# Two wq matrices loaded by one DMA of 96 rows each, in a two-problem decode attention kernel

## The chip, the cores and the metric

One core of one Trainium2 chip runs the whole kernel. The metric is device microseconds of one execution, as the median of several. A profiled execution gives a page and a trace; its span begins and ends a little inside the time of that execution.

## The reference, cut to what matters

Two independent problems, A and B, have the same shapes; their outputs are laid side by side. Everything is bf16.

```python
B, Sq, D = 2, 1, 576
Hq, Hkv, Sk, Dh = 32, 16, 16384, 128
W = min(4096, max(256, Sk // 4))             # 4096
q = (x @ wq)                                 # wq is 576 x 4096; 2 batches, 32 heads of 128
k = k_cache[:, :, Sk - W:, :]                # the last 4096 rows, each kv head shared by 2 q heads
v = v_cache[:, :, Sk - W:, :]
p = softmax(q k^T * Dh ** -0.5)
return (p v) @ wo                            # wo is 4096 x 576
```

For each problem that is 2 x 16 caches of 4096 x 128 for K and as many for V, wq of 4.7 MB and wo of 4.7 MB: 153 MB to read in all, with two rows of x per problem against them.

## The kernel before, in words

The kernel is a list of operations written in Python and emitted in order, engine by engine; each operation names those it depends on, and a small planner turns that into semaphore waits. The engines are PE (matmuls), DVE, ACT, POOL and SP; SP issues nearly all DMAs, in order, and waits in that order too.

**Slabs.** Four kv heads' worth of K (or V) make a slab: 128 partitions of 32768 bytes, 4 MB. There are 16 slabs of K and 16 of V. They go through a ring of four slots in SBUF (`ring`, `NR = 4`), one DMA each. The order is the list `stream`: wq of A, wq of B, K0, K1, V0, K2, V1 and so on (V13 is the one slab moved, and the last V slab comes in two pieces). Stream element n takes slot n mod 4, and its DMA (L256) waits for the last reader of element n - 4. So V0 waits for the last matmul of q that reads wq of A, K2 for the last that reads wq of B, V1 for the last transpose of K0. The weights wo come in parts between slabs (L291), the last ones (L277) at the very end of the queue.

**wq and x.** 576 rows of wq are cut into 512 and 64. The 512 go into a ring slot as 128 partitions of 4 rows (L265). The 64 go into `wqr` (L263), each row cut into two halves so that 128 partitions of 4096 bytes are filled. x of A is loaded from ACT's queue, x of B from SP's, behind wq of A. L380 doubles the 64 rest columns of x, five matmuls at L375 transpose x (4 rows) into a PSUM bank, L389 (ACT) and L397 (DVE, with the mask maskP of L382) write it, spread into a zeroed tile, to `xT`, which holds the stationary operands of q.

**q.** `do_qpair` (L425 to L456) makes q for two groups at a time into four PSUM banks: per pair 16 matmuls of 128x512 on the ring slot and four on `wqr` (a matmul's line is L450, or the helper's L188 where the stationary operand is kept). There are four pairs, 80 matmuls. Per group, ACT copies the row out (L465 or L470), DVE transposes it (L475), ACT keeps it (L483).

**Per slab pair.** DVE transposes each K slab in four parts into one of three buffers `xt` (L515), PE makes scores from it (L540), then come maximum, exponential (ACT, L585), and a transpose of the weights (L593). PE multiplies them with the V slab (L631) into the bank `ACC`; ACT evicts that to `acc_sb` (L643). For all groups but the last, POOL folds the evicted slab in three steps (mask L650, add L653, add L658) and a matmul per slab (L671) sums over partitions. In the last group (slabs 14 and 15) there is no fold: four matmuls per slab sum it (L678). DVE scales the result, redistribution and projection matmuls (L786, L790) finish it. Softmax sums go through `rsel` (POOL, L600).

**The end.** After slab 13, the list has: sum of slab 13, projection of a group (L786, eight pairs), redistribution, sum of slab 14, another projection of eight pairs, then the two pieces of the last V slab (L631), its sum, its projection with the last weights (L790), and output.

**Small parts.** Masks are reduced from a 128x128 identity, which POOL makes (L207, L208); L213 makes it in fp32. The tiles that only the q phase needs (`early`) share SBUF with the second half of `wob`, the place of wo.

Of the kernel before, what the change touches and what calls it, by code (L numbers as in the profile page):

```python
# [59 lines left out]
def build_kernel(nc, probs, out, cfg=None):  # L60
# [25 lines left out]
    NFC = D // 128  # L86
    DREM = D - 128 * NFC
    assert DREM * 2 == 128 and NFC * HD == SLABW
    HH = HD // 2
    NXC = NFC + 2  # L90
# [23 lines left out]
    with es:  # L114
        sb = lambda name, shape, dt: es.enter_context(nc.sbuf_tensor(name, shape, dt))
        ring = sb("ring", [128, NR, SLABW], BF16)
        xt = sb("xt", [128, NKT, 2048], FP32)
        wob = sb("wob", [128, NSW, NOUT], BF16)
        used = [0]

        def early(shape):
            n = 1
            for d_ in shape:
                n *= d_
            a = wob[:, NSW // 2:NSW, :].rearrange("p s n -> p (s n)")[:, used[0]:used[0] + n]
            used[0] += n
            assert used[0] <= NSW // 2 * NOUT
            names = "abc"[:len(shape)]
            return a if len(shape) == 1 else a.rearrange("p (%s) -> p %s" % (" ".join(names), " ".join(names)), **dict(zip(names, shape)))
        wqr = early([NPROB, HH])  # L130
        qrow = early([1024])
        qtr = early([1024])
        xT = early([NXC, NPROB, 128])
        x_sb = early([D])[0:NPROB * Bb]
        x_dup = early([DREM, 2])[0:NPROB * Bb]
# [20 lines left out]
        masks = sb("masks", [128, 30], BF16)  # L156
        maskS, mask16D, maskA, mask4S, maskJ, maskP = (masks[:, a_:b_] for a_, b_ in ((0, 8), (8, 16), (16, 20), (20, 24), (24, 28), (28, 30)))
# [21 lines left out]
        wq_sem = sem("wq")  # L179
# [22 lines left out]
        def load_x(P, eng):  # L202
# [4 lines left out]
        p_ones_b = S.add("pool", lambda e: e.memset(ones_b[:], 1.0), [], "ones_b")  # L207
        p_ident_b = S.add("pool", lambda e: e.affine_select(ident_b[:], ones_b[:], [[-1, 128]], ALU.is_equal, 0.0,  # L208
                                                           base=0, channel_multiplier=1), [p_ones_b], "ident_b")
        p_zxT = S.add("dve", lambda e: e.memset(xT[:].rearrange("c h p w -> c (h p w)").bitcast(FP32), 0.0), [], "zero_xT")  # L210
        p_zq = S.add("dve", lambda e: e.memset(zq[:].rearrange("d p z w -> d (p z w)").bitcast(FP32), 0.0), [], "zero_zq")
        p_ones_f = S.add("dve", lambda e: e.memset(ones_f[:], 1.0), [], "ones_f")
        p_ident_f = S.add("pool", lambda e: e.affine_select(ident_f[:], ones_f[:], [[-1, 128]], ALU.is_equal, 0.0,  # L213
                                                           base=0, channel_multiplier=1), [p_ones_f], "ident_f")
# [13 lines left out]

        slab_dma = {}
        pieces = []  # L230
        reader = {}
        wq_dma = {}
# [6 lines left out]
        def issue_slab(n):  # L239
# [7 lines left out]
            r = n % NR  # L247
# [11 lines left out]
        def issue_wq(n, P):  # L259
            wqP = probs[P][3]  # L260
            r = n % NR
            deps = [reader[n - NR]] if n >= NR else []
            wq_dma[P] = dma_op("sp", wq_sem, 1, lambda e: e.dma_start(  # L263
                wqr[:, P, :], wqP[NFC * 128:D, :].rearrange("r (h n) -> r h n", h=2)).then_inc(wq_sem, 16), [], "wqr%d" % P)
            slab_dma[n] = dma_op("sp", ring_sem[r], 1, lambda e: e.dma_start(  # L265
                ring[:, r, :], wqP[0:NFC * 128, :].rearrange("(p s) n -> p (s n)", s=NFC)).then_inc(ring_sem[r], 16), deps, "wq%d" % P)

            if P == 0:
                for P_ in range(1, NPROB):
                    x_dma[P_] = load_x(P_, "sp")  # L270
# [96 lines left out]
        def f_xT(e, bank):  # L367
            last = None
            NB = NPROB * Bb
            for ch in range(NFC + 1):  # L370
                if ch < NFC:
                    src = x_sb[0:NB, 0:NFC * 128].rearrange("b (p s) -> b s p", s=NFC)[:, ch, :]
                else:
                    src = x_dup[0:NB, :, :].rearrange("b r t -> b (r t)")
                last = e.matmul(bank[:, ch * 4 * NB:(ch + 1) * 4 * NB], src, ident_b[0:NB, 0:NB].rearrange(  # L375
                    "k (p b) -> k p b", b=Bb).unsqueeze(2).broadcast_to([NB, NPROB, 4, Bb]), start=True, stop=True)
            return last
        issue_until(0)
        init_small()
        x_cd = S.add("dve", lambda e: e.tensor_copy(  # L380
            x_dup[:], x_sb[:, NFC * 128:D].unsqueeze(2).broadcast_to([NPROB * Bb, DREM, 2])), list(x_dma.values()), "xdup")
        init["maskP"] = S.add("dve", lambda e: e.tensor_reduce(  # L382
            maskP[:], ident_b[:].rearrange("d (r t) -> d t r", t=2), AX.X, ALU.max), [p_ident_b], "maskP")

        n_x, bank_x, op_xT = tb_job(f_xT, "xT", list(x_dma.values()) + [x_cd, p_ident_b])

        def f_xev(e):
            NB = NPROB * NFC * 4
            return e.activation(  # L389
                xT[:, 0:NFC].rearrange("c h p (a w) -> c (h p a) w", a=4)[:, :, 0:Bb],  # L390
                bank_x[:, 0:NB * Bb].rearrange("c (q b) -> c q b", b=Bb),
                ACTF.Copy)
        op_xev = S.add("act", f_xev, [op_xT, p_zxT], "xev")
        NB_ = NPROB * 4 * Bb

        def f_xev2(e):
            return e.tensor_tensor(  # L397
                xT[:, NFC:NXC].rearrange("c h p (a w) -> c h (p a) w", a=4)[:, :, :, 0:Bb],
                bank_x[:, NFC * NB_:(NFC + 1) * NB_].rearrange("c (q b) -> c q b", b=Bb).unsqueeze(1).broadcast_to([128, 2, NPROB * 4, Bb]),
                maskP[:].unsqueeze(2).unsqueeze(3).broadcast_to([128, 2, NPROB * 4, Bb]), ALU.mult)  # L400
        op_xev = S.add("dve", f_xev2, [op_xev, op_xT, init["maskP"]], "xev2")
        tb_consumer[n_x] = op_xev

# [20 lines left out]
        def do_qpair(i):  # L424
# [5 lines left out]
            mine = lambda ch: [b for b in range(4) if ch < NFC or b % 2 == ch - NFC]  # L430
            order = [NFC, NFC + 1] + list(range(NFC))
            if Gs[0] % GPP:
                order = order[::-1]
            todo_ = [(ch, b) for ch in order for b in mine(ch)]
# [4 lines left out]
            for g in range(2):  # L439
                def fn(e, part=todo_[(0, ends[0])[g]:ends[g]]):  # L440
                    last = None
                    for ch, b in part:
                        c0 = (b % 2) * HH + 512 * (Gs[b // 2] % GPP)
                        w_ = ring[:, nq % NR, ch * HD + c0:ch * HD + c0 + 512] if ch < NFC else wqr[:, P, c0 - (b % 2) * HH:c0 - (b % 2) * HH + 512]
                        start, stop = seen[b] == 0, seen[b] == NFC
                        seen[b] += 1
                        if q_first[0] == (P, ch):
                            last = matmul_again(e, q_first[1], banks[b], w_, start, stop, False)
                        else:
                            last = q_first[1] = e.matmul(banks[b], xT[:, ch, P, :], w_, start=start, stop=stop)  # L450
                            q_first[0] = (P, ch)
                    return last
                before = [q_free.get((i - 1, b)) for b in range(4)] if g else []
                op = S.add("pe", fn, [slab_dma[nq], op_xev] + list(wq_dma.values()) + prev + before, "q%d" % Gs[g])
# [53 lines left out]
        def do_X(s, u):  # L508
# [4 lines left out]
            if i >= NKT:  # L513
                deps.append(Sop[divmod(i - NKT, NU)])
            Xop[(s, u)] = S.add("dve", lambda e: e.transpose(  # L515
                xt[:, i % NKT, :].rearrange("k (j w) -> k j w", w=64),
                ring[:, n % NR, :].bitcast(FP32).rearrange("k (j q w) -> k q j w", q=4, w=64)[:, u]),
# [78 lines left out]
        def do_rsel(G):  # L596
            d = [chain[(2 * G, "exp")], chain[(2 * G + 1, "exp")], init["maskS"]]
            if G >= 1:
                d.append(chain[(G - 1, "tot")])
            chain[(G, "rsel")] = S.add("pool", lambda e: e.tensor_tensor(  # L600
# [17 lines left out]
        def do_PV(D_, rounds, wait):  # L618
# [7 lines left out]
            def f(e):  # L626
                last = None
                for jr in rounds:
                    for cb in range(4):
# [3 lines left out]
                                        ring[:, n % NR, j0_ * 128:(j0_ + 4) * 128],  # L633
# [5 lines left out]
            if rounds[-1] == last_r:  # L639
# [5 lines left out]
                if not by_group(G) or (D_ % 2 == 0 and G < NG - 2):  # L645
                    return
                l0, l1 = (0, 2) if G < NG - 2 else (D_ % 2, D_ % 2 + 1)
                a_ = acc_sb[:, l0:l1, :]
                v = a_.rearrange("k l (j d) -> k l j d", j=4)
                t = S.add("pool", lambda e: e.tensor_tensor(  # L650
                    v, v, maskJ[:].unsqueeze(1).unsqueeze(3).broadcast_to([128, l1 - l0, 4, 128]), ALU.mult),
                    [acc_ev[2 * G + l] for l in range(l0, l1)] + [init["maskJ"]], "accm%d" % D_)
                t = S.add("pool", lambda e: e.tensor_tensor(a_[:, :, 0:256], a_[:, :, 0:256], a_[:, :, 256:512], ALU.add),  # L653
                          [t], "acca%d" % D_)
                d = [t]
                if G >= 1:
                    d.append(comb[2 * G - 1])
                t = S.add("pool", lambda e: e.tensor_tensor(  # L658
                    acc_r[:, l0:l1, :], a_[:, :, 0:128], a_[:, :, 128:256], ALU.add), d, "accr%d" % D_)
                for l in range(l0, l1):  # L660
                    acc_r_ev[2 * G + l] = t

        def do_comb(D_):
            if by_group(D_ // 2):
# [8 lines left out]
                n, bank, comb[D_] = tb_job(fg, "comb%d" % D_, [acc_r_ev[D_ - 1], acc_r_ev[D_], init["maskS"]])  # L673
            else:
# [230 lines left out]
        do_comb(D_)  # L905
        do_norm(D_)
# [117 lines left out]
```

## Time and profile before

| what | value |
|---|---|
| median of 3 runs | 362.77 us (362.70 to 362.87) |
| the profiled execution | 363.02 us |
| its span | 361.8 us |
| busy: PE, DVE, ACT, POOL | 218.6, 200.9, 68.2, 35.3 us |
| DMA read | 153.10 MB, 423 GB/s over the span |
| queue q1 | 6476 packets, 98.8% of 16 engines' span |
| first wq issue, first V issue | 0.79 us, 26.99 us |
| last weights landed | 359.71 us |

Busy time is per engine; engines overlap. A DMA is cut into packets, here one per row of a partition, and these are shared over sixteen DMA engines, each with its own line of packets to work off. The DMA row of the page gives, for 40 equal slices of the span, how full these engines are, in tenths. The chain of waits is followed back from the last instruction: at each step to what released it. A landing mark in the trace is the moment at which one DMA engine reports its share of a transfer done.

### The profile page before, as it was taken

To read this page: it belongs to the slowest core of one execution; us is meant where nothing else is said; L and a number is where in the kernel's file an instruction comes from. 1 tells how busy PE (TensorE), PEld (TensorE's weight loads), DVE (VectorE), ACT (ScalarE), POOL (GpSimd) and SP (SyncE) were. 2 spreads that over 40 slices of the span, in tenths; PEclk is the share of its full clock that TensorE was granted. 3 is DMA by queue.
4 is the path that set the end of the run, shared out by engine and by line. 5 is a ranking of instruction groups with operands and counts; after the bars stand their busy time and mean duration, and the time that the engine had idled before them with its cause. 6 is when DMAs were issued, how large, how long until landed. Compare 5 with 4: busy or idle time off the path is not lost.

```text
span 361.8 us, 2730 instructions
## 1 busy us (share of the span) xinstructions
PE 218.6 (60%) x1318; PEld 55.8 (15%) x945; DVE 200.9 (56%) x175; ACT 68.2 (19%) x149; POOL 35.3 (10%) x55
## 2 busy tenths in 40 slices
PE   0399195763747207466574737766867707657786
PEld 0010021120111101112120201212121201211132
DVE  4112599846647019283756658392919239079931
ACT  1036502130203002103020203020201203002131
POOL 1000000004000400001300040002100040200020
PEclk9999689997889857969698978899898978969999
DMA  8999999999999999999999999999999999999996
GB/s 348 421 449 406 464 406 437 431 408 453 415 442 438 428 424 438 429 428 438 417 446 422 435 428 442 426 435 428 424 424 440 431 424 433 431 438 428 438 409 248
DMA packets 6491, 153.27 MB, mean 424 GB/s; under 512 B 712, under 2 KB 1232, under 8 KB 1616
## 3 DMA queue, kind: packets, MB, share of 16 engines
q1 hardware_dynamic: 6476, 153.10, 98.8%
q8 instruction: 9, 0.15, 0.2%
q14 instruction: 2, 0.02, 0.0%
q10 hardware_dynamic: 4, 0.00, 0.0%
HBM read 153.10 MB, written 0.00 MB: 423 GB/s over the span
## 4 chain that ended last, share of the span: by engine, by line
DMA 72%; DVE 17%; PE 7%; ACT 3%; SPq 1%; issue 0%
DMA ring<-in_B_k_cache_dram 34%; DMA ring<-in_A_k_cache_dram 27%; DVE xt L515 14%; DMA wob<-in_B_wo_dram 8%; DMA wob<-in_B_x_dram 3%; PE st L188 3%; PE st L540 3%; ACT wob L465 1%; DVE wob L475 1%; ACT qk L483 1%; PE st L450 1%; DVE m L550 1%; ACT wob L470 1%; DVE nM L563 0%; SPq L252 0%
## 5 line engine op out<-in xcount | busy, mean ns | idle before, releaser
L515 DVE STREAM_TRANSPOSE xt<-ring 128x2048 f32<-128x2048 f32 x64 | 145.3, 2284 | 86.6 <-DMA ring<-in_A_k_cache_dram 49.8
L540 PE MATMUL st<-xt,zq 128*128 128x512 bf16 x256 | 111.6, 436 | 122.6 <-DVE xt L515 98.1
L188 PE MATMUL st<-xt,zq 128*128 128x512 bf16 x256 | 110.1, 430 | 0.0
L540 PEld LDWEIGHTS st<-xt,zq 128*128 128x128 bf16 x256 | 27.1, 106 | 216.3 <-DVE xt L515 113.5
L631 PE MATMUL acc<-ring,pC 128*32 128x512 bf16 x512 | 32.5, 381 | 1.2 <-DMA ring<-in_B_v_cache_dram 1.2
L568 ACT ACTIVATE nMrep<-nM 1x128 f32<-1x128 f32 x16 | 4.9, 308 | 146.9 <-DVE nM L563 146.9
L643 ACT ACTIVATE acc_sb<-acc 128x512 bf16<-128x512 f32 x16 | 9.5, 596 | 79.9 <-PE acc L631 79.9
L593 DVE STREAM_TRANSPOSE pC<-pR 128x1024 bf16<-128x1024 bf16 x16 | 19.6, 1223 | 3.7 <-ACT pR L585 2.1
L650 POOL TENSOR_TENSOR acc_sb<-acc_sb,masks 128x1024 bf16<-128x1024 bf16 (+1 forms) x8 | 13.4, 1679 | 66.6 <-ACT acc_sb L643 66.6
L550 DVE TENSOR_REDUCE m<-st 128x1 f32<-128x1024 f32 x16 | 19.0, 1190 | 1.4 <-PE st L188 1.4
L502 POOL TENSOR_TENSOR zq<-qk,masks 128x128 bf16<-128x128 bf16 x16 | 6.3, 398 | 136.2 <-PE st L188 114.4
L585 ACT ACTIVATE pR<-st,bias_sb 128x1024 bf16<-128x1024 f32 x16 | 17.8, 1114 | 0.5
L475 DVE STREAM_TRANSPOSE wob<-wob 128x512 f32<-128x512 f32 x8 | 5.7, 711 | 20.3 <-ACT wob L465 12.9
L415 ACT ACTIVATE st<-maskB 128x1024 f32<-128x1024 bf16 x16 | 16.5, 1032 | 1.6 <-POOL rsel L600 0.4
L786 PE MATMUL ot<-wob,Rsb 128*2 128x512 bf16 x56 | 15.2, 390 | 0.0
L631 PEld LDWEIGHTS acc<-ring,pC 128*32 128x32 bf16 x512 | 12.4, 96 | 15.9 <-issue 3.2
L600 POOL TENSOR_TENSOR rsel<-masks,rsum 128x16 f32<-128x16 bf16 x8 | 1.7, 216 | 108.0 <-ACT pR L585 108.0
L188 PE MATMUL tb<-wob,Rsb 128*2 128x64 bf16 x56 | 10.9, 195 | 0.0
L375 PE MATMUL tb<-wob 4*128 4x16 bf16 x5 | 0.3, 179 | 14.5 <-DVE wob L380 14.5
L653 POOL TENSOR_TENSOR acc_sb<-acc_sb 128x512 bf16<-128x512 bf16 (+1 forms) x8 | 8.2, 1029 | 0.6
L188 PE MATMUL st<-ring,wob 128*128 128x512 bf16 x24 | 7.9, 445 | 0.0
L579 ACT ACTIVATE bias_sb<-tb 128x1 f32<-128x1 f32 x16 | 2.7, 171 | 24.8 <-PE tb L573 24.8
(89 smaller groups left out, 99.5 us busy)
## 6 DMA issues: line engine op xcount, KB each, us to landing
ring<-in_A_k_cache_dram SPq DMA_DIRECT2D x8, 4096.0 KB, 30.4
ring<-in_A_v_cache_dram SPq DMA_DIRECT2D x8, 4096.0 KB, 32.5
ring<-in_B_k_cache_dram SPq DMA_DIRECT2D x8, 4096.0 KB, 28.4
ring<-in_B_v_cache_dram SPq DMA_DIRECT2D x7, 4096.0 KB, 32.8
wob<-in_A_wo_dram SPq DMA_DIRECT2D x1, 4608.0 KB, 43.3
ring<-in_A_wq_dram SPq DMA_DIRECT2D x1, 4096.0 KB, 12.7
ring<-in_B_wq_dram SPq DMA_DIRECT2D x1, 4096.0 KB, 22.6
ring<-in_B_v_cache_dram SPq DMA_DIRECT2D x1, 3072.0 KB, 25.5
```

The costliest lines, as they stand in the source:

```text
L188: return e.add_instruction(mybir.InstMatmult(name=nc.get_next_instruction_name(), engine=i.engine, ins=[e.lower_ap(rhs), i.ins[1]], outs=[ ...
L415: chain[(s, "fill")] = S.add("act", lambda e: e.activation(ST[s % 2][:, :].rearrange("k (h j) -> k h j", h=2), maskB[:].unsqueeze(1).broad ...
L475: chain[(G, "qtr")] = S.add("dve", lambda e: e.transpose(qtr[:].bitcast(FP32), qrow[:].bitcast(FP32)), evs, "qtr%d" % G)
L515: Xop[(s, u)] = S.add("dve", lambda e: e.transpose(xt[:, i % NKT, :].rearrange("k (j w) -> k j w", w=64), ring[:, n % NR, :].bitcast(FP32) ...
L540: first = last = e.matmul(bank, zq[:, p4, s % NZQ, w0:w0 + 128], mv, start=False, stop=stop, skip_group_check=True)
L550: chain[(s, "max")] = S.add("dve", lambda e: e.tensor_reduce(m1[:, 0:1], ST[s % 2][:, :], AX.X, ALU.max), d, "max%d" % s)
L585: chain[(s, "exp")] = S.add("act", lambda e: e.activation(pR[:, :], ST[s % 2][:, :], ACTF.Exp, bias=bias_sb[:, 0:1], scale=SCALE, accum_ou ...
L593: chain[(s, "pC")] = S.add("dve", lambda e: e.transpose(pC[:, s % NPT, :, :].rearrange("k j c -> k (j c)"), pR[:, :]), d, "pC%d" % s)
L631: last = e.matmul(ACC[32 * cb:32 * cb + 32, 0:512], pC[:, D_ % NPT, j0_:j0_ + 4, :].rearrange("k j c -> k (j c)"), ring[:, n % NR, j0_ * 1 ...
L643: acc_ev[D_] = S.add("act", lambda e: e.activation(acc_sb[:, D_ % 2, :], ACC[:, :], ACTF.Copy), d, "accev%d" % D_)
L650: t = S.add("pool", lambda e: e.tensor_tensor(v, v, maskJ[:].unsqueeze(1).unsqueeze(3).broadcast_to([128, l1 - l0, 4, 128]), ALU.mult), [a ...
L786: first = e.matmul(OT[0:Bb, 0:NB0], l_, wob[:, w0 + s_, 0:NB0], start=start and begin, stop=end, skip_group_check=True)
```

## The change

wq of a problem comes by a single DMA: 576 = 96 x 6, so 96 partitions of 6 rows, 49152 bytes each, in place of 128 partitions of 32768 and 128 of 4096. As a row is now wider than a ring slot, `xt`, `ring` and `wob` become one tile `big`: wq of A lies over slot 0 and the end of `xt` ahead of it, wq of B over slot 3 and the start of `wob` behind it; the slots are taken in the order 0, 3, 1, 2. The first three transposes of K0 into `xt` also wait for the last reader of wq of A.

q sums six products of 96 rows: 24 matmuls per pair, 96 in all, with contraction over 96 partitions.

x is turned without PE: ACT copies its rows apart (`x_s`), DVE transposes 32 x 192 three times (`x_t`), ACT spreads it into `xT`, once per problem. `x_dup`, maskP and the five matmuls go.

Slab 14's accumulator is folded by POOL, in place, with the same three steps as the others; one matmul in place of four sums it.

Three small operations leave POOL: ones_b goes to DVE, the fp32 identity is copied by ACT, and the first group's `rsel` is made by two ACT operations.

```diff
-    NFC = D // 128
+    NFC = 6
+    DP = D // NFC
+    EXT = NFC * HD - SLABW
+        RING0 = NKT * 4096
+        WOB0 = RING0 + NR * SLABW
+        big = sb("big", [128, WOB0 + NSW * NOUT], BF16)
...
+        wqv = [big[0:DP, RING0 - EXT:RING0 + SLABW], big[0:DP, WOB0 - SLABW:WOB0 + EXT]]
...
-        p_ones_b = S.add("pool", lambda e: e.memset(ones_b[:], 1.0), [], "ones_b")
+        p_ones_b = S.add("dve", lambda e: e.memset(ones_b[:], 1.0), [], "ones_b")
+        p_zxs = S.add("dve", lambda e: e.memset(x_s[:].rearrange("b s p -> b (s p)").bitcast(FP32), 0.0), [], "zero_xs")
-        p_ident_f = S.add("pool", lambda e: e.affine_select(ident_f[:], ones_f[:], [[-1, 128]], ALU.is_equal, 0.0,
-                                                           base=0, channel_multiplier=1), [p_ones_f], "ident_f")
+        p_ident_f = S.add("act", lambda e: e.activation(ident_f[:], ident_b[:], ACTF.Copy), [p_ident_b], "ident_f")
...
+        slot = [(0, 3, 1, 2)[n % NR] for n in range(len(stream))]
...
-            wq_dma[P] = dma_op("sp", wq_sem, 1, lambda e: e.dma_start(
-                wqr[:, P, :], wqP[NFC * 128:D, :].rearrange("r (h n) -> r h n", h=2)).then_inc(wq_sem, 16), [], "wqr%d" % P)
             slab_dma[n] = dma_op("sp", ring_sem[r], 1, lambda e: e.dma_start(
-                ring[:, r, :], wqP[0:NFC * 128, :].rearrange("(p s) n -> p (s n)", s=NFC)).then_inc(ring_sem[r], 16), deps, "wq%d" % P)
+                wqv[P], wqP.rearrange("(p s) n -> p (s n)", s=NFC)).then_inc(ring_sem[r], 16), [], "wq%d" % P)
...
+        x_cp = S.add("act", lambda e: e.activation(
+            x_s[0:NB], x_sb[:, :].rearrange("b (p s) -> b s p", s=NFC), ACTF.Copy), list(x_dma.values()) + [p_zxs], "xcp")
+        for i_ in range(DP // 32):
+            op_xt = S.add("dve", lambda e, i_=i_: e.transpose(
+                x_t[32 * i_:32 * i_ + 32], x_s[:, :, 32 * i_:32 * i_ + 32]), [x_cp], "xtr%d" % i_)
+        for P_ in range(NPROB):
+            op_xev = S.add("act", lambda e, P_=P_: e.activation(
+                xT[0:DP, :, P_].rearrange("c h (a w) -> c h a w", a=4)[:, :, :, 0:Bb],
+                x_t[:, :, Bb * P_:Bb * P_ + Bb].unsqueeze(2).broadcast_to([DP, NFC, 4, Bb]), ACTF.Copy), [op_xt, p_zxT], "xev%d" % P_)
...
-            order = [NFC, NFC + 1] + list(range(NFC))
+            order = list(range(NFC))
...
-            todo_ = [(ch, b) for ch in order for b in mine(ch)]
+            todo_ = [(ch, b) for ch in order for b in range(4)]
...
-                            last = q_first[1] = e.matmul(banks[b], xT[:, ch, P, :], w_, start=start, stop=stop)
+                            last = q_first[1] = e.matmul(banks[b], xT[0:DP, ch, P, :], w_, start=start, stop=stop)
...
-            if i >= NKT:
-                deps.append(Sop[divmod(i - NKT, NU)])
+            deps.append(Sop[divmod(i - NKT, NU)] if i >= NKT else reader[pos[("Q", 0)]])
...
+            if G == 0:
+                for l in range(2):
+                    chain[(G, "rsel")] = S.add("act", lambda e, l=l: e.activation(
+                        rsel[:, l, :], maskS[:], ACTF.Copy, scale=rsum[:, l:l + 1]), d, "rsel%d_%d" % (G, l))
+                return
...
+            elif D_ < ND - 1:
+                n, bank, comb[D_] = tb_job(lambda e, bank: e.matmul(
+                    bank[:, 0:8], acc_sb[:, 0, 0:128], maskS[:, :], start=True, stop=True), "comb%d" % D_, [acc_r_ev[D_], init["maskS"]])
...
         do_comb(D_)
+        do_fold(ND - 2, 0, 1)
         do_norm(D_)
```

`do_fold` holds the three POOL steps that stood in `do_PV`.

More of the change, by code (lines that the diff above doesn't have):

```diff
@@ L85, in build_kernel @@
     GPP = SPP // 2
-    NFC = D // 128
-    DREM = D - 128 * NFC
-    assert DREM * 2 == 128 and NFC * HD == SLABW
+    NFC = 6
+    DP = D // NFC
     HH = HD // 2
-    NXC = NFC + 2
+    EXT = NFC * HD - SLABW
+    assert D == DP * NFC and DP % 16 == 0 and 0 < EXT <= 2 * 4096
     NOUT = wo0.shape[1]
@@ L115, in build_kernel @@
         sb = lambda name, shape, dt: es.enter_context(nc.sbuf_tensor(name, shape, dt))
[L116 to L119, printed above, removed]
+        RING0 = NKT * 4096
+        WOB0 = RING0 + NR * SLABW
+        big = sb("big", [128, WOB0 + NSW * NOUT], BF16)
+        xt = big[:, 0:RING0].bitcast(FP32).rearrange("k (n w) -> k n w", n=NKT)
+        ring = big[:, RING0:WOB0].rearrange("k (n w) -> k n w", n=NR)
+        wob = big[:, WOB0:WOB0 + NSW * NOUT].rearrange("k (s n) -> k s n", n=NOUT)
+        wqv = [big[0:DP, RING0 - EXT:RING0 + SLABW], big[0:DP, WOB0 - SLABW:WOB0 + EXT]]
+        used = [EXT]
         def early(shape):
@@ L124, in early @@
                 n *= d_
-            a = wob[:, NSW // 2:NSW, :].rearrange("p s n -> p (s n)")[:, used[0]:used[0] + n]
+            a = big[:, WOB0 + used[0]:WOB0 + used[0] + n]
             used[0] += n
-            assert used[0] <= NSW // 2 * NOUT
+            assert used[0] <= NSW * NOUT
             names = "abc"[:len(shape)]
             return a if len(shape) == 1 else a.rearrange("p (%s) -> p %s" % (" ".join(names), " ".join(names)), **dict(zip(names, shape)))
-        wqr = early([NPROB, HH])
         qrow = early([1024])
         qtr = early([1024])
-        xT = early([NXC, NPROB, 128])
+        xT = early([NFC, NPROB, 128])
         x_sb = early([D])[0:NPROB * Bb]
-        x_dup = early([DREM, 2])[0:NPROB * Bb]
+        x_s = early([NFC, DP])[0:32]
+        x_t = early([NFC, 32])[0:DP]
         ident_b = early([128])
@@ L155, in build_kernel @@
         Rsb = [sb("Rsb%d" % n_, [128, Bb, n], BF16) for n_, n in enumerate((32, 16))]
-        masks = sb("masks", [128, 30], BF16)
-        maskS, mask16D, maskA, mask4S, maskJ, maskP = (masks[:, a_:b_] for a_, b_ in ((0, 8), (8, 16), (16, 20), (20, 24), (24, 28), (28, 30)))
+        masks = sb("masks", [128, 28], BF16)
+        maskS, mask16D, maskA, mask4S, maskJ = (masks[:, a_:b_] for a_, b_ in ((0, 8), (8, 16), (16, 20), (20, 24), (24, 28)))
         mask16S = sb("mask16S", [128, 16], BF16)
@@ L178, in build_kernel @@
         ring_sem = [sem("ring%d" % r) for r in range(NR)]
-        wq_sem = sem("wq")
         wo_sem = [sem("wo%d" % r) for r in range(2)]
@@ L231, in build_kernel @@
         reader = {}
-        wq_dma = {}
         wo_dma = {}
@@ L246, in issue_slab @@
             src = src_t.rearrange("b h s d -> (b h) s d")[g::SPP, Sk - W:Sk, :].rearrange("c (r j) d -> r c (j d)", r=32)
-            r = n % NR
+            r = slot[n]
             deps = [reader[n - NR]] if n >= NR else []
@@ L260, in issue_wq @@
             wqP = probs[P][3]
-            r = n % NR
-            deps = [reader[n - NR]] if n >= NR else []
-            wq_dma[P] = dma_op("sp", wq_sem, 1, lambda e: e.dma_start(
-                wqr[:, P, :], wqP[NFC * 128:D, :].rearrange("r (h n) -> r h n", h=2)).then_inc(wq_sem, 16), [], "wqr%d" % P)
+            r = slot[n]
             slab_dma[n] = dma_op("sp", ring_sem[r], 1, lambda e: e.dma_start(
-                ring[:, r, :], wqP[0:NFC * 128, :].rearrange("(p s) n -> p (s n)", s=NFC)).then_inc(ring_sem[r], 16), deps, "wq%d" % P)
+                wqv[P], wqP.rearrange("(p s) n -> p (s n)", s=NFC)).then_inc(ring_sem[r], 16), [], "wq%d" % P)
             if P == 0:
@@ L365, in init_small @@
                 ident_r[:], ident_b[:].rearrange("d (a r) -> d r a", a=4), AX.X, ALU.max), [p_ident_b], "ident_r")
[L367 to L377, printed above, removed]
@@ L378, in build_kernel @@
         issue_until(0)
         init_small()
[L380 to L401, printed above, removed]
@@ L402, in build_kernel @@
-        tb_consumer[n_x] = op_xev
+        NB = NPROB * Bb
+        x_cp = S.add("act", lambda e: e.activation(
[7 more added lines that the diff above has]
+                x_t[:, :, Bb * P_:Bb * P_ + Bb].unsqueeze(2).broadcast_to([DP, NFC, 4, Bb]), ACTF.Copy), [op_xt, p_zxT], "xev%d" % P_)
@@ L429, in do_qpair @@
             banks = q_banks(i)
-            mine = lambda ch: [b for b in range(4) if ch < NFC or b % 2 == ch - NFC]
-            order = [NFC, NFC + 1] + list(range(NFC))
+            order = list(range(NFC))
             if Gs[0] % GPP:
                 order = order[::-1]
-            todo_ = [(ch, b) for ch in order for b in mine(ch)]
+            todo_ = [(ch, b) for ch in order for b in range(4)]
             seen = {b: 0 for b in range(4)}
@@ L442, in fn @@
                     for ch, b in part:
-                        c0 = (b % 2) * HH + 512 * (Gs[b // 2] % GPP)
-                        w_ = ring[:, nq % NR, ch * HD + c0:ch * HD + c0 + 512] if ch < NFC else wqr[:, P, c0 - (b % 2) * HH:c0 - (b % 2) * HH + 512]
-                        start, stop = seen[b] == 0, seen[b] == NFC
+                        c0 = ch * HD + (b % 2) * HH + 512 * (Gs[b // 2] % GPP)
+                        w_ = wqv[P][:, c0:c0 + 512]
+                        start, stop = seen[b] == 0, seen[b] == NFC - 1
                         seen[b] += 1
@@ L453, in do_qpair @@
                 before = [q_free.get((i - 1, b)) for b in range(4)] if g else []
-                op = S.add("pe", fn, [slab_dma[nq], op_xev] + list(wq_dma.values()) + prev + before, "q%d" % Gs[g])
+                op = S.add("pe", fn, [slab_dma[nq], op_xev] + prev + before, "q%d" % Gs[g])
                 reader[nq] = op
@@ L512, in do_X @@
             deps = [slab_dma[n]]
-            if i >= NKT:
-                deps.append(Sop[divmod(i - NKT, NU)])
+            deps.append(Sop[divmod(i - NKT, NU)] if i >= NKT else reader[pos[("Q", 0)]])
             Xop[(s, u)] = S.add("dve", lambda e: e.transpose(
                 xt[:, i % NKT, :].rearrange("k (j w) -> k j w", w=64),
-                ring[:, n % NR, :].bitcast(FP32).rearrange("k (j q w) -> k q j w", q=4, w=64)[:, u]),
+                ring[:, slot[n], :].bitcast(FP32).rearrange("k (j q w) -> k q j w", q=4, w=64)[:, u]),
                 deps, "X%d_%d" % (s, u))
@@ L632, in f @@
                                         pC[:, D_ % NPT, j0_:j0_ + 4, :].rearrange("k j c -> k (j c)"),
-                                        ring[:, n % NR, j0_ * 128:(j0_ + 4) * 128],
+                                        ring[:, slot[n], j0_ * 128:(j0_ + 4) * 128],
                                         start=(jr == 0), stop=(jr == last_r))
@@ L644, in do_PV, with do_fold @@
                 G = D_ // 2
[L645 to L661, printed above, removed]
+                if G < NG - 2 and D_ % 2:
+                    do_fold(D_, 0, 2)
+                elif G == NG - 2:
+                    do_fold(D_, D_ % 2, D_ % 2 + 1)
+        def do_fold(D_, l0, l1):
+            G = D_ // 2
+            a_ = acc_sb[:, l0:l1, :]
+            v = a_.rearrange("k l (j d) -> k l j d", j=4)
+            t = S.add("pool", lambda e: e.tensor_tensor(
+                v, v, maskJ[:].unsqueeze(1).unsqueeze(3).broadcast_to([128, l1 - l0, 4, 128]), ALU.mult),
+                [acc_ev[2 * G + l] for l in range(l0, l1)] + [init["maskJ"]], "accm%d" % D_)
+            t = S.add("pool", lambda e: e.tensor_tensor(a_[:, :, 0:256], a_[:, :, 0:256], a_[:, :, 256:512], ALU.add),
+                      [t], "acca%d" % D_)
+            d = [t]
+            if 1 <= G < NG - 1:
+                d.append(comb[2 * G - 1])
+            o_ = acc_r[:, l0:l1, :] if by_group(G) else a_[:, :, 0:128]
+            t = S.add("pool", lambda e: e.tensor_tensor(
+                o_, a_[:, :, 0:128], a_[:, :, 128:256], ALU.add), d, "accr%d" % D_)
+            for l in range(l0, l1):
+                acc_r_ev[2 * G + l] = t
         def do_comb(D_):
```

## The prediction

> **What bounds the kernel now.** I read the page first, its second and third parts.
>
> ```profile
> span 361.8 us, 2730 instructions
> ...
> DMA  8999999999999999999999999999999999999996
> GB/s 348 421 449 406 464 406 437 431 408 453 415 442 438 428 424 438 429 428 438 417 446 422 435 428 442 426 435 428 424 424 440 431 424 433 431 438 428 438 409 248
> ...
> q1 hardware_dynamic: 6476, 153.10, 98.8%
> ```
>
> The DMA row is at nine tenths or more in all slices but the first and the last, and the packets of queue q1 fill 98.8% of sixteen engines' span, 0.988 x 361.8 = 357.5 us. Nothing else is near: PE 60%, DVE 56%. So a compute edit is worth nothing while the queue stays filled, and whatever lengthens the busiest engine's packets is paid in full. The end confirms it, in the chain of waits:
>
> ```profile
> 331.87 27.84 DMA wob<-in_B_wo_dram
> 359.71 0.04 issue
> 359.75 0.31 PE st L790 x2
> 360.06 0.02 issue
> 360.08 0.45 DVE pR L823
> ```
>
> The last weights, issued 27.84 us earlier, land at 359.71; 0.04 + 0.31 + 0.02 + 0.45 us of work and the output DMA follow. Time is (first packet) + (packets of the slowest engine) + (this tail).
>
> Third, SP's timeline shows how long the queue runs on if a slab is issued late:
>
> ```profile
> 0.79 0.40 SPq L263 DMA_DIRECT2D wob<-in_A_wq_dram  x1
> ...
> 1.72 0.31 SPq L203 DMA_DIRECT2D wob<-in_B_x_dram  x1
> ...
> 3.00 1.26 SPq L256 DMA_DIRECT2D ring<-in_A_k_cache_dram  x2
> 26.99 0.54 SPq L256 DMA_DIRECT2D ring<-in_A_v_cache_dram  x1
> 36.04 0.54 SPq L256 DMA_DIRECT2D ring<-in_A_k_cache_dram  x1
> 50.67 0.54 SPq L256 DMA_DIRECT2D ring<-in_A_v_cache_dram  x1
> ```
>
> By the trace's landing marks the second K slab is in at 44.43, V0 at 54.14 and K2 at 63.93. So V0, issued at 26.99, had 17.4 us to spare; K2 (36.04) 18.1 us; V1 (50.67) 13.3 us.
>
> **The wq load.** The trace's packet records give the price by size: 4096 B take 159 ns, 32768 B 1215 ns (medians), 36864 B 1364 ns, a semaphore packet 9 ns. From the smallest to the largest that is (1364 - 159) / 32768 = 0.0368 ns per byte, so 49152 B take 1364 + 12288 x 0.0368 = 1816 ns (an estimate). A problem's wq is now 128 packets of 32768 B and 128 of 4096 B, on each engine 8 x (1215 + 159) + 2 x 9 = 11010 ns. Afterwards it is 96 packets; six on each engine, if evenly shared, are 6 x 1816 + 9 = 10905 ns. Two problems: -0.21 us. The bytes are the same.
>
> Nothing in the trace shows a big load on fewer than 128 partitions, so this share is bounded from both sides. Below: -0.21 us and up to 0.1 us of the slow first packets (the 256 of 4096 B average 176 ns against 159, most of that the first arrival, which stays), so -0.3. Above: every packet at half pace, 6 x 1816 more per problem, +21.8 us. [...] The nearest row is the second x load, two rows in neighbouring partitions: its landing marks are two, at 13.69 and 14.18 us, so neighbours went to two engines, by count and not by place. I take the even split.
>
> [...]
>
> **The head.** Two small issues leave SP's queue (0.40 and 0.34 us of issuing), but the first big one takes the place of the first small one at 0.79, so the first packet (1.71 us) does not move: 0. The x of B stays behind the first wq and lands at about 14.1. What follows it now costs, in the chain,
>
> ```profile
> 14.20 0.23 DVE wob L380
> ...
> 14.47 0.34 PE tb L375 x5
> ...
> 14.83 0.23 ACT wob L389
> ...
> 15.09 0.20 DVE wob L397
> ...
> 15.42 0.59 PE st L450
> ```
>
> 1.24 us from landing to q's first matmul. Afterwards: a copy on ACT of 4 x 576, about 0.64 us (the 128x512 ones take 0.59, the 128x1024 ones 1.01); three DVE transposes of 32 x 192 bf16, at most 3 x 0.36 (the 128x1024 bf16 one takes 1.22); two ACT copies of 48 elements at 0.22 (the 64-element one). That is 2.2 us with gaps, +0.9. Then q has 24 matmuls per pair of groups in place of 20. The first 14 matmuls run at 0.43 us, the rest at 0.216, with the granted clock 1.00 throughout; 16 more cost 16 x 0.216 = 3.5 us in all, 8 x 0.216 = 1.7 of it ahead of V0's issue and at most 3.5 ahead of K2's. So V0 goes out some 2.6 us later and K2 up to 4.4: hidden by the 17.4 and 18.1 us above. V1 waits for DVE's transposes of K0, which begin after the q chain; 4.4 of its 13.3 us go. The new wait of the first transposes on q's second pair is nothing: q ends near 30, the transposes of K0 begin near 42. If that cover were gone, the price would be the delay, up to 4.4 us.
>
> POOL, DVE and ACT trades (ones_b, a memset of 128x288 f32, ident_f, the first rsel as two ACT rows of about 0.2 us instead of one POOL row of 0.22): before 14 us all three wait for x, and rsel falls at 74.35 us with two whole slabs still queued (issued at 61.36 and 66.57). 0.
>
> **The tail.** Slab 14's fold puts three POOL rows between its eviction and its sum. The row pattern is slab 13's:
>
> ```profile
> 346.92 1.04 POOL L650 TENSOR_TENSOR acc_sb<-acc_sb,masks 128x512 bf16<-128x512 bf16 x1 [0.27 <-ACT acc_sb L643]
> ...
> 348.04 0.67 POOL L653 TENSOR_TENSOR acc_sb<-acc_sb 128x256 bf16<-128x256 bf16 x1
> ...
> 348.79 0.42 POOL L658 TENSOR_TENSOR acc_r<-acc_sb 128x128 bf16<-128x128 bf16 x1
> ```
>
> From 346.92 to the matmul that uses it (349.27) 2.35 us pass. Slab 14's eviction ends at 349.04 + 0.60 = 349.64, so its matmul can start at 349.71 + 2.35 = 352.06; it stood at 351.92. Queued behind it on PE are eight pairs of projection matmuls, to 354.2, then the last slab's PV, which waits for its first piece until 354.34 and idles 1.01 us before the second piece at 356.87. So +0.14 us, up to 0.6 if DVE's 0.43 us mask product blocks POOL, go into that idle time: 0. Three matmuls fewer save 0.2 us of the same idle time: 0.
>
> **Sum.** -0.21 - 0.05 (middle of 0 to 0.1). The profiled execution took 363.02 us, its span 361.8 and 1.2 around it; 363.02 - 0.26 = 362.76. The median shown is 362.77, 0.25 below that execution: 362.5.
>
> **Rivals.**
>
> [...] 362.77 + 7.05 = 369.8. [...] Chance 27%.
>
> *The paths also collide.* If engines that meet on one path stay in step, packets run at half pace for longer; between 7 and the 21.8 us above, 372 to 384. Against it: the longest 32768 B packet of the trace takes 1.75 us, and the marks of whole slabs stay 0.5 us apart early on. 12%.
>
> *A late q phase or fold reaches the end.* The price is 4.4 us at the most, 0.5 likelier. Against it: covers of 9 us and more in the head, 1 us in the tail. 6%.
>
> *The load is not one packet per row.* The largest seen is 36864 B. Halved rows would add 12 x 9 ns: within my forecast.
>
> *More is gained.* The sixteen last marks lie between 357.81 and 359.71; if the late engines are relieved by chance, 0.8 to 1.5 us, 361.3 to 362.0. 7%.
>
> **How the numbers follow.** Forecast 48%, 362.5, its own range 362.0 to 363.3. What this kernel's measurement can tell from no change is about 0.2%, 0.73 us, so the forecast counts as the same. Slower 27 + 12 + 6 = 45%, faster 7%. The range runs from 362.0 to 371.5: it takes in the first rival and leaves out the collisions (12%) and the chance gain (7%).
>
> **What would show it.** Right: 6124 packets on q1 (6476 less 256 of 4096 B, 64 big ones and 2 x 16 semaphore packets), its share at 98.8% still, wq of A landed by 14.1 and of B by 25, V0 issued near 29.6, the second slice at 420 GB/s. [...] Wrong by the tail: a POOL row ending later than the PV's first piece. A matmul of V's last piece released by something other than its DMA would overturn the reasoning on covers.

## The result and the profile after

The changed kernel takes 385.15 us (384.81 to 385.69, 6 runs) against 362.76 us (362.63 to 362.87) for the kernel before: a ratio of 1.062, 95% interval 1.0606 to 1.0634. That is 22.4 us more, outside the range of the forecast. The profiled execution took 385.23 us with a span of 384.0.

The page of the changed kernel, the parts that were read first in the forecast:

```profile
span 384.0 us, 2734 instructions
...
DMA  9897999999999999999999999999999999999996
GB/s 236 174 246 164 263 420 420 427 435 434 434 437 432 439 437 422 427 423 428 437 430 437 435 430 430 427 435 427 427 432 430 434 416 445 434 437 427 430 418 251
...
q1 hardware_dynamic: 6124, 153.10, 98.8%
```

Three things are to be seen. The packets are 6124, as counted, and the bytes the same. The DMA row is as full as before. But for the first five slices (48 us) the GB/s row stands at 164 to 263 where it stood at 348 to 464: the engines are busy, and move about half as much. After that the two kernels are alike.

By stretches: from and to, length, the busy us and the count of PE, of its weight loads, of DVE, ACT and POOL, then PE's granted clock, the DMA share and GB/s (1.00 is a full share; a packet counts where it starts):

```profile
2.00:25.00 23.00, 0.00 (x0) 0.00 (x0) 3.09 (x13) 0.96 (x2) 0.00 (x0) 1.00 1.02 216
25.00:47.00 22.00, 13.78 (x48) 1.29 (x11) 4.66 (x9) 7.56 (x25) 0.76 (x2) 0.96 0.92 203
47.00:60.00 13.00, 12.40 (x48) 1.19 (x11) 1.42 (x2) 3.70 (x10) 0.00 (x0) 0.81 0.98 421
```

The issue lists say the same of each load; the last column is the time from issue to landing. First the larger part of each wq in the kernel before, then each wq after:

```profile
ring<-in_A_wq_dram SPq DMA_DIRECT2D x1, 4096.0 KB, 12.7
ring<-in_B_wq_dram SPq DMA_DIRECT2D x1, 4096.0 KB, 22.6
...
big<-in_A_wq_dram SPq DMA_DIRECT2D x1, 4608.0 KB, 24.5
big<-in_B_wq_dram SPq DMA_DIRECT2D x1, 4608.0 KB, 46.0
```

By the packet records, the 192 packets of 49152 bytes took 3.70 us on average (3.08 to 4.02), where the forecast had 1.816. The sum closes: 12 packets per engine x (3.696 - 1.816) - 0.21 = +22.35 us, and the measured ratio's interval is 22.0 to 23.0 us. The 192 packets start in twelve groups of sixteen, 3.1 to 3.8 us apart, which fits one packet on each engine per group. All sixteen engines were equally late: the landing marks of wq of A lie within 0.8 us (24.57 to 25.34).

The rest of the program shifted behind it. SP's timeline:

```profile
0.79 0.38 SPq L265 DMA_DIRECT2D big<-in_A_wq_dram  x1
...
1.59 0.32 SPq L265 DMA_DIRECT2D big<-in_B_wq_dram  x1
1.95 1.25 SPq L259 DMA_DIRECT2D big<-in_A_k_cache_dram  x2
42.18 0.54 SPq L259 DMA_DIRECT2D big<-in_A_v_cache_dram  x1
60.35 0.53 SPq L259 DMA_DIRECT2D big<-in_A_k_cache_dram  x1
74.08 0.54 SPq L259 DMA_DIRECT2D big<-in_A_v_cache_dram  x1
```

V0 is issued at 42.18, but K1 lands at 66.8 by its last landing mark, so the queue never ran dry. The end of the chain of waits:

```profile
380.82 1.11 PE st L777 x14
381.94 0.03 issue
381.97 0.31 PE st L777 x2
382.30 0.45 DVE pR L810
```

The chain now ends through PE, without the wait for the last weights. Their last landing mark is at 381.92, where that PE work ends: the two are level. In the timeline PE's last two groups of weight loads, at 381.65 and 381.96, still waited 0.24 and 0.23 us for those weights. From the last mark to the end of the span are 2.05 us, as before.

### The profile page after: what moved, and what is told of

It reads as the page before. It is cut to its first block, busy times and chain, and to the rows that moved or that the text cites. A ratio compares the mean times of both kernels' runs of the same rounds, so it can differ in the third digit from the quotient of the medians.

```text
span 384.0 us, 2734 instructions
## 1 busy us (share of the span) xinstructions
PE 227.5 (59%) x1325; PEld 56.5 (15%) x937; DVE 201.9 (53%) x177; ACT 70.3 (18%) x154; POOL 36.8 (10%) x55
## 3 DMA queue, kind: packets, MB, share of 16 engines
q1 hardware_dynamic: 6124, 153.10, 98.8%
## 4 chain that ended last, share of the span: by engine, by line
DMA 66%; DVE 15%; PE 14%; ACT 2%; POOL 1%; issue 0%; SPq 0%
DMA big<-in_B_k_cache_dram 23%; DMA big<-in_A_k_cache_dram 23%; DVE big L489 13%; DMA big<-in_B_wq_dram 12%; DMA big<-in_B_v_cache_dram 8%; PE st L191 5%; PE st L514 4%; PE acc L610 2%; PE ot L773 1%; DVE big L450 1%; DVE m L524 1%; PE st L425 1%; ACT big L440 1%; ACT big L445 1%; ACT st L391 0%; ACT qk L458 0%
## 5 line engine op out<-in xcount | busy, mean ns | idle before, releaser
L489 DVE STREAM_TRANSPOSE big<-big 128x2048 f32<-128x2048 f32 x64 | 145.3, 2284 | 83.4 <-DMA big<-in_A_k_cache_dram 48.2
L514 PE MATMUL st<-big,zq 128*128 128x512 bf16 x256 | 112.8, 441 | 117.9 <-DVE big L489 93.1
L191 PE MATMUL st<-big,zq 128*128 128x512 bf16 x256 | 110.9, 433 | 0.0
L514 PEld LDWEIGHTS st<-big,zq 128*128 128x128 bf16 x256 | 27.3, 107 | 212.8 <-DVE big L489 107.8
L610 PE MATMUL acc<-big,pC 128*32 128x512 bf16 x512 | 34.3, 395 | 0.5 <-DMA big<-in_B_v_cache_dram 0.5
L425 PE MATMUL st<-big 96*128 96x512 bf16 x12 | 6.3, 522 | 33.8 <-ACT big L376 28.4
L450 DVE STREAM_TRANSPOSE big<-big 128x512 f32<-128x512 f32 x8 | 5.7, 712 | 31.0 <-ACT big L440 23.0
L633 POOL TENSOR_TENSOR acc_sb<-acc_sb,masks 128x1024 bf16<-128x1024 bf16 (+1 forms) x9 | 14.5, 1612 | 77.8 <-ACT acc_sb L622 77.8
L773 PE MATMUL ot<-big,Rsb 128*2 128x512 bf16 x56 | 15.9, 402 | 0.0
L610 PEld LDWEIGHTS acc<-big,pC 128*32 128x32 bf16 x512 | 13.0, 98 | 15.6 <-issue 4.5
L191 PE MATMUL st<-big 96*128 96x512 bf16 x36 | 14.0, 514 | 0.0
L373 DVE STREAM_TRANSPOSE big<-big 32x192 bf16<-32x192 bf16 x3 | 1.1, 368 | 21.6 <-ACT big L370 21.5
L191 PE MATMUL tb<-big,Rsb 128*2 128x64 bf16 x56 | 11.1, 199 | 0.0
```

Of the source, the lines that this page charges most:

```text
L191: return e.add_instruction(mybir.InstMatmult(name=nc.get_next_instruction_name(), engine=i.engine, ins=[e.lower_ap(rhs), i.ins[1]], outs=[ ...
L425: last = q_first[1] = e.matmul(banks[b], xT[0:DP, ch, P, :], w_, start=start, stop=stop)
L450: chain[(G, "qtr")] = S.add("dve", lambda e: e.transpose(qtr[:].bitcast(FP32), qrow[:].bitcast(FP32)), evs, "qtr%d" % G)
L489: Xop[(s, u)] = S.add("dve", lambda e: e.transpose(xt[:, i % NKT, :].rearrange("k (j w) -> k j w", w=64), ring[:, slot[n], :].bitcast(FP32 ...
L514: first = last = e.matmul(bank, zq[:, p4, s % NZQ, w0:w0 + 128], mv, start=False, stop=stop, skip_group_check=True)
L610: last = e.matmul(ACC[32 * cb:32 * cb + 32, 0:512], pC[:, D_ % NPT, j0_:j0_ + 4, :].rearrange("k j c -> k (j c)"), ring[:, slot[n], j0_ * ...
```

## The experiments

Two microkernels load and compute nothing else; five kernels are variants of the two that are compared. Each microkernel ran once. Times of loads are from the packet records, from the first packet's start to the last one's end. A load alone has its first arrival in it: 128 rows took 1.1 to 1.3 us more than eight packets' median price, so the GB/s below are lower than in a full queue.

**Which property of the load is it?** The microkernel `loads` issues one load at a time, each waited for, from a list of (source, first partition, rows, elements per row):

```python
nc.sync.dma_start(slots[i % n_slot][p0:p0 + n, 0:w], src).then_inc(sems[i], 16)
nc.sync.wait_ge(sems[i], 16)
```

The theories are COUNT and LENGTH, as worded below, and PLACE: that a load's time goes by the partitions its rows lie in.

> This kernel computes nothing: its output is zeros. It makes 17 loads one after the other, each waited for: 128, 112, 96, 80, 64, 48, 32 and 16 rows from partition 0 of 32768 bytes, 96 rows of 49152 and 24576 bytes, 128 and 64 rows of 49152, 128 of 36864, 96 rows from partition 32, 64 rows from partition 64, and 96 rows of 32768 bytes whose sources lie 65536 bytes apart. What is read is the time of a packet. Three theories. COUNT (96 rows, six on an engine, are the trouble, whatever their length): every 96-row load has packets at twice the price by length, 2.43 us for 32768 bytes and 1.83 for 24576, also from partition 32 and from spaced sources; 128 rows of 49152 bytes run at 1.82; 64, 32 and 16 rows at 1.22. LENGTH (rows over 36864 bytes are the trouble): 49152 bytes take 3.7 us on 128, 96 and 64 rows alike; everything shorter runs at the price of before, 1.22 for 32768 and 0.92 for 24576. [...]

| load | packets' median, us | times the price by length | GB/s |
|---|---|---|---|
| 128 rows of 32768 B | 1.21 | 1.0 | 387 |
| 128 rows of 49152 B | 1.82 | 1.0 | 402 |
| 128 rows of 36864 B | 1.36 | 1.0 | 388 |
| 112 rows of 32768 B | 2.09 | 1.7 | 250 |
| 96 rows of 49152 B (wq; the cache) | 3.76; 3.73 | 2.1 | 205; 207 |
| 96 rows of 32768 B | 2.37 | 1.9 | 206 |
| 96 rows of 24576 B | 1.74 | 1.9 | 208 |
| 96 rows, sources 65536 B apart | 2.45 | 2.0 | 209 |
| 96 rows from partition 32 | 2.37 | 2.0 | 207 |
| 80 rows | 2.41 | 2.0 | 208 |
| 64 rows from 0; from 64 | 2.56; 2.56 | 2.1 | 200; 194 |
| 64 rows of 49152 B | 3.84 | 2.1 | 199 |
| 48 rows | 3.94 | 3.2 | 132 |
| 32 rows | 2.56 | 2.1 | 188 |
| 16 rows | 3.67 | 3.0 | 122 |

SP's timeline of this run shows it for rows of 49152 bytes. Each load is issued once the one before has landed, so the distance of two lines is the time of the first, with issue and landing in it:

```profile
12.91 0.34 SPq L50 DMA_DIRECT2D slot<-in_B_k_cache_dram  x1
29.88 0.34 SPq L50 DMA_DIRECT2D slot<-in_A_wq_dram  x1
54.31 0.32 SPq L50 DMA_DIRECT2D slot<-in_B_k_cache_dram  x1
```

128 rows take 16.97 us, the 96 rows of wq 24.43, for three quarters of the bytes.

The length of a row is out: 128 rows of 49152 bytes run at the price by length, 96 rows of 24576 to 49152 bytes do not. So is the source's spacing: packets of 2.45 us with it, 2.37 without. COUNT is out as worded: 64, 32 and 16 rows are slow too. On PLACE this run does not decide: 64 rows take 2.56 us from 0 and from 64, 96 rows 2.37 from 0 and from 32. And 48 rows (3.94) are slower than 32 (2.56).

**Do the small parts of the change cost anything?** The kernel before with only them:

```diff
-        p_ones_b = S.add("pool", lambda e: e.memset(ones_b[:], 1.0), [], "ones_b")
+        p_ones_b = S.add("dve", lambda e: e.memset(ones_b[:], 1.0), [], "ones_b")
...
+        do_fold(ND - 2, 0, 1)
         do_norm(D_)
```

> The kernel before with only the small parts of the change: slab 14's fold on GpSimd, ones_b on VectorE, the fp32 identity and the first rsel on ScalarE. wq, x and q as before. All three theories lay the whole loss on the wq load and expect 362.8 us, within 0.2. The rival that the fold or the moved operations cost part of the 22.4 us expects 363.3 or more.

Measured: 363.2 us against 362.83, ratio 1.0004 (0.9995 to 1.0014): no difference. The median lies between the two expectations, and the interval reaches 0.5 us, so a cost of some tenths is not ruled out; a larger part of the 22.4 us is. The chain of waits of this kernel still ends through the last weights, as before:

```profile
331.01 28.27 DMA wob<-in_B_wo_dram
359.28 0.04 issue
```

**Shorter rows in the kernel.** The changed kernel with each wq load in two halves along the row:

```diff
...
-                wqv[P], wqP.rearrange("(p s) n -> p (s n)", s=NFC)).then_inc(ring_sem[r], 16), [], "wq%d" % P)
+            for h in range(2):
+                c0, c1 = h * NFC * HD // 2, (h + 1) * NFC * HD // 2
...
+                    wqv[P][:, c0:c1], wqP.rearrange("(p s) n -> p (s n)", s=NFC)[:, c0:c1]).then_inc(wq_sem[2 * P + h], 16), [], "wq%d_%d" % (P, h))
```

> The changed kernel with each wq load cut into two loads of 96 rows of 24576 bytes, one after the other; all else as changed. COUNT: still double, packets of 1.83 us, 385 us. LENGTH: packets of 0.92 us, the loss is gone, 362.9 us. PLACE: rows and partitions are the same as in the change, so 385 us.

Measured: 383.48 us, ratio 1.0567 (1.0552 to 1.0581). LENGTH is out in the kernel as well. Packets of 24576 bytes took 1.77 us; 24 of them are 42.6 us per engine against 44.4 for the change's twelve, which is about the 1.7 us by which it is faster. Why halves fare that little better was not looked into.

**A cut at partition 64.** The same cut along the partitions:

```diff
...
-                wqv[P], wqP.rearrange("(p s) n -> p (s n)", s=NFC)).then_inc(ring_sem[r], 16), [], "wq%d" % P)
+            for h in range(2):
+                c0, c1 = ((0, 64), (64, 96))[h]
...
+                    wqv[P][c0:c1, :], wqP.rearrange("(p s) n -> p (s n)", s=NFC)[c0:c1, :]).then_inc(wq_sem[2 * P + h], 16), [], "wq%d_%d" % (P, h))
```

> The changed kernel with each wq load cut into a load of partitions 0 to 63 and one of 64 to 95, rows of 49152 bytes as in the change. COUNT: four and two rows on an engine, powers of two, so packets of 1.82 us and 362.9 us. LENGTH: packets of 3.7 us, 385 us. [...]

Measured: 386.72 us, ratio 1.066 (1.0646 to 1.0675). COUNT fails again. LENGTH comes near with 385, but the other runs have ruled it out. An estimate from the prices of `loads` comes near too: on each engine, if the rows are evenly shared, 4 x 3.84 us for the 64 rows and 2 x 2.1 x 1.816 for the 32, 23.0 us per problem against 11.01, gives 386.7 us.

**Where rows start.** In `loads` only two loads of 32768-byte rows start elsewhere than at partition 0. COUNT now says that fewer than 128 rows run at half pace wherever they lie; what is left beside it is that the first partition matters. The microkernel `starts` is `loads` with another list.

> This kernel computes nothing: its output is zeros. 13 loads, one after the other, that differ in the partition they start at; rows of 32768 bytes but for one of 49152. [...] COUNT (fewer than 128 rows run at half pace wherever they lie): 64 from 32 as from 0, 9.7.

SP's timeline of this run carries it, read as above; a distance is 1.4 to 2.3 us more than the load's own time by the packet records (10.93, 10.57 and 5.80 us), for issue and landing.

```profile
0.73 0.40 SPq L46 DMA_DIRECT2D slot<-in_A_k_cache_dram  x1
13.03 0.54 SPq L46 DMA_DIRECT2D slot<-in_B_k_cache_dram  x1
25.86 0.53 SPq L46 DMA_DIRECT2D slot<-in_A_k_cache_dram  x1
33.32 0.51 SPq L46 DMA_DIRECT2D slot<-in_B_k_cache_dram  x1
```

128 rows take 12.30 us, 64 rows from partition 0 take 12.83, no less for half the bytes, and 64 rows from partition 32 take 7.46. The source is not the reason: `loads` put the same 64 rows of A's cache at partitions 0 to 63 in 10.51 us, and here they go to 32 to 95 in 5.80. All loads of the run with fewer than 128 rows:

| load | at the price by length, us | at twice that, us | measured, us |
|---|---|---|---|
| 64 from 0 | 4.9 | 9.7 | 10.57 |
| 64 from 32 (twice) | 4.9 | 9.7 | 5.80; 5.98 |
| 64 of 49152 B from 32 | 7.3 | 14.5 | 8.86 |
| 64 from 16 | 4.9 | 9.7 | 10.52 |
| 96 from 16 | 7.3 | 14.6 | 15.34 |
| 48 from 0 | 3.6 | 7.3 | 12.14 |
| 48 from 40 | 3.6 | 7.3 | 7.43 |
| 32 from 0; from 48 | 2.4 | 4.9 | 5.51; 5.54 |
| 112 from 8 | 8.5 | 17.0 | 16.22 |
| 16 from 0 | 1.2 | 2.4 | 4.13 |

The second and third columns are estimates: the rows evenly shared over sixteen engines, at 1.215 us a packet (1.816 for 49152 bytes), without the first arrival.

COUNT is out: 64 rows run at the full price, packets of 1.21 us, from partition 32, and at double from partitions 0 and 16. The first partition matters for 48 rows as well: 12.14 us from 0, 7.43 from 40. The number of rows matters beside it: 48 rows from 0 take longer than 64 (10.57).

**A cut at partition 32.** The cut at 64 moved to partition 32, so that 64 rows start where they run at the full price in `starts` (against that run):

```diff
-                c0, c1 = ((0, 64), (64, 96))[h]
+                c0, c1 = ((0, 32), (32, 96))[h]
```

CROWD, in the text below, is the author's reckoning of which loads are slowed; no run shows the layout that it assumes. For this kernel it comes to prices that were measured: double for the 32 rows from 0 (`loads`, packets of 2.56 us for 1.21), single for the 64 from 32 (`starts`, 1.21).

> The changed kernel with each wq load cut into a load of partitions 0 to 31 and one of 32 to 95, rows of 49152 bytes: the same rows in the same places as with the cut at 64, which took 386.7 us. CROWD: two rows per engine at double and four at single price, 2 x 3.63 + 4 x 1.82 = 14.5 us per problem against 11.0 before: 369.9 us. COUNT: 385 us, as both loads have fewer than 128 rows. Packets should be 64 of 3.6 us and 128 of 1.82 us under CROWD.

Measured: 371.61 us, ratio 1.0241 (1.0227 to 1.0255). The same rows at the same places, cut 32 partitions lower, run 15.1 us faster. The page:

```profile
GB/s 213 383 250 402 439 411 450 420 433 442 403 451 436 409 447 432 427 439 411 453 432 416 435 435 432 434 414 450 435 418 423 439 414 445 435 428 435 425 421 241
```

The second slice, where the 64 rows of A go, is at 383, between two slow ones. Packets there settle at 1.82 us; in the step in which the slow load passes into the fast one they take 2.0 to 3.0. That is most of the 1.7 us over CROWD's 369.9. The packets of the slow loads took 3.7 us, as in the change.

**All but the load.** The changed kernel, with the load's shape alone altered (the view `wqv` and the matmuls' slices of it follow):

```diff
...
-                wqv[P], wqP.rearrange("(p s) n -> p (s n)", s=NFC)).then_inc(ring_sem[r], 16), [], "wq%d" % P)
+                wqv[P], wqP.rearrange("r n -> (r n)").rearrange("(p f) -> p f", p=128)).then_inc(ring_sem[r], 16), [], "wq%d" % P)
...
```

> The changed kernel with all its other parts (x turned by VectorE, 96 matmuls of 96 rows, fold, moved operations), but each wq loaded flat by one load of 128 rows of 36864 bytes, so that the matmuls multiply x with the wrong weights: q is not the reference's, and every operation and its size is the change's. If the whole loss is the 96-row load: 8 x 1.364 us of packets per problem, 362.6 us, within 0.3. If 16 more matmuls, the longer way of x or the wait of the first transposes cost anything: 363.5 or more.

Measured: 363.07 us against 362.85, ratio 1.0007 (0.9998 to 1.0016). That is above the 362.3 to 362.9 expected with no other cost, and below the 363.5 expected with one. 96 matmuls, the new way of x, the wait of the first transposes, the fold: together nothing that can be told from zero, and at most some tenths. SP's timeline shows the delays that were hidden:

```profile
29.35 0.54 SPq L259 DMA_DIRECT2D big<-in_A_v_cache_dram  x1
39.71 0.54 SPq L259 DMA_DIRECT2D big<-in_A_k_cache_dram  x1
53.44 0.54 SPq L259 DMA_DIRECT2D big<-in_A_v_cache_dram  x1
```

V0, K2 and V1 go out 2.4, 3.7 and 2.8 us later than in the kernel before, all within the 13 us and more of queued transfers. The 0.2 us that the packets were to save does not show either. No run points to a version faster than the kernel before.

## Why the prediction was wrong

**What bounds the kernel: right.** The time followed the packets of the DMA engines (22.35 us worked out from packets, 22.39 measured, interval 22.0 to 23.0), and no compute edit moved it by more than the noise.

**The wq load: wrong, and all of the miss.** The failing step is "I take the even split", with its term 6 x 1816: six packets of 1.816 us on each engine. The first half of it held: by the groups of sixteen and the landing marks there are six packets on each engine, all equally loaded. The second did not: the price of a packet was taken to go by its length alone, and it was 3.696 us. The step rested on the two landing marks of x (13.69 and 14.18 us), which show that neighbouring rows go to different engines. I read that as a sign that place does not matter. The marks were of two tiny rows and said nothing of the price of big packets.

The term was bounded from above at half pace for every packet, 21.8 us more, and it landed there, 0.6 us above the bound: a packet took 3.70 us, a little over twice 1.816. The forecast chose the other end because the nearest rows were even; but all big rows of the trace were loads of 128 partitions, and could not tell what fewer cost. The range was given an end (371.5) that left the second rival out.

**The rivals.** "The paths also collide", at 372 to 384 with 12%, comes nearest: the time is 385.15 us, and every packet ran at about half pace (3.08 to 4.02 us for 1.816). That paths are shared, and that engines meet on them, was the author's assumption; no run shows it. What was held against this rival, that no packet in the trace is that slow, was no evidence, for the reason above. The 7.05 us of the first rival, with 27%, no run shows either: the loss is 22.4 us, and no engine ran ahead, with none of 192 packets under 3.08 us and the landing marks of wq of A within 0.8 us.

**The head: right in its covers, off in its rows.** The copy of x on ACT took 0.96 us for 0.64, the three transposes 1.17 for 1.08. In the kernel with the flat load V0 went out 2.4 us later (2.6 forecast), K2 3.7 (up to 4.4). All hidden, as said. The 2.4 us come near by luck: x landed 0.26 us earlier, its way to the first matmul took 1.49 us longer (0.9 forecast), and from there to V0's issue 1.13 us more passed (1.7 forecast). K2's landing was read one mark short, 63.93 for 65.06, which makes V1's spare time 14.4 us and changes nothing.

**The tail: the size right, the cover thinner than said.** From slab 14's eviction (372.78 + 0.60) to its matmul (375.82) passed 2.44 us; 2.42 was forecast. The up to 0.6 us for a mask product of DVE that blocks POOL no run shows: the first product ran from 373.19 to 373.61, the fold's first row from 373.45 for 1.07 us, where slab 13's took 1.04. In the changed kernel PE then waited 0.72 us for it:

```profile
375.82 0.18 PE L659 MATMUL tb<-masks,acc_sb 128*128 128x8 bf16 x1 [0.72 <-POOL acc_sb L642]
```

It began the last slab's first piece at 377.41, 0.85 us after that had landed. This is the sign that I had named against the covers. It still cost nothing that can be seen: PE caught up and finished level with the last weights, and with the other small parts the fold is within noise (`small_parts`).

## What to carry to other kernels

Before changing how many partitions a big load spans, measure that load alone: where every load of a kernel has 128 rows, its profile cannot tell what another count costs. Here only the 128-row loads, and 64 rows from partition 32, ran at full pace (packets of 1.21 us for 32768 bytes); 96 rows cost about double from partitions 0, 16 and 32 alike (packets of 2.37 us from 0 and 32; 15.34 us for the load from 16, 7.3 at the price by length), and 64 rows cost double or single by their first partition (10.57 us from 0, 10.52 from 16, 5.80 from 32). In this kernel, whose DMA queue is always full (98.8%), such a load is paid to the last microsecond (22.35 us by its packets, 22.39 measured), while sixteen matmuls more cost nothing that can be told from noise (`flat_128`, 363.07 us against 362.85).

## What the runs showed of the hardware

The packets' busy share does not tell that a load is slow: in the changed kernel's stretches it was 0.92 to 1.02 at 203 to 216 GB/s, and 0.98 at 421. GB/s beside it does.

A load's time does not go by its bytes alone, but by how many rows it has and where they lie: 64 rows took as long as 128 (10.57 and 10.93 us), 48 longer than 64 (12.14 and 10.57), 64 from partition 32 half as long (5.80).

The cut at partition 32 took 371.61 us where 369.9 was expected, so the prices of single loads carry over to the kernel. No run shows which engine writes which row, or what slows it. What stays open: why a load's pace goes by the number and the place of its rows, why all sixteen engines are slowed alike (landing marks within 0.8 us), and why 48 rows from 0 cost three times the price by length (3.94 us) where 112 cost 1.7 times (2.09).
